# Weight preparation six tiles deep with the third block's attention behind it, and five of the first expert's eight weight pieces behind its gathered rows

## The chip, the cores and the metric

The kernel runs on one NeuronCore of a Trainium2 chip. The metric is the device time of one execution in microseconds (us). The times below are medians of several runs of the same program; the profile is of one more execution. The engines are named as in the profile: PE is TensorE (PEld its weight loads), DVE is VectorE, ACT is ScalarE, POOL is GpSimd and SP is SyncE, which here does nothing but issue DMAs; ACTq and SPq are the DMA issues of ACT and SP.

## What is computed

Three layers follow each other, all in float32 accuracy. The first is gated linear attention, the second a feed-forward layer, the third a mixture of eight experts in which every expert takes exactly 384 of the 3072 tokens:

```python
f = 1.0 / (1.0 + np.exp(-f_logit))                      # 4 batches, 8 heads, 768 steps, 48 wide
for t in range(S):
    state = f[:, :, t, :, None] * state + np.einsum('bhd,bhe->bhde', k[:, :, t], v[:, :, t])
    y[:, :, t] = np.einsum('bhd,bhde->bhe', q[:, :, t], state)
...
h = x @ w_in                                            # 3072 tokens, 384 -> 2048
x = (np.maximum(h, 0) + alpha * np.minimum(h, 0)) @ w_out
...
logits = x @ w_gate                                     # 8 experts, at most N // 8 tokens each
for idx in np.argsort(-logits.flatten()):               # best (token, expert) pairs first
    ...
out[mask] = np.maximum(x[mask] @ w1[e], 0) @ w2[e]      # 384 -> 1024 -> 384
```

## The kernel before

The 3072 tokens are 24 chunks of 128, and three chunks are a block. Attention is done by chunk (`chunk`): on DVE two scans over 128x516 elements (`s1`), two products of 128x512 (`s2`), two maskings of 128x512 (`s3`) and a few small operations; on PE short matmuls between them; the result is a block's input in two halves, high and low (`halve_x`). The feed-forward (`ffn1`) runs by block: for each of 16 hidden chunks nine matmuls (`hidden`), an activation on ACT and DVE, a split into a high and a low half (`split`: ACT rounds, DVE or POOL subtracts), and two chunks later nine matmuls of the projection (`project`). Every product is made of three matmuls (high by low, low by high, high by high).

The weights of the feed-forward come as 64-bit numbers, and are narrowed to 32 bits on the core before they are split: `load_w` loads group g (of 8) into two raw buffers with four DMAs of 384 KB; `prepare_in` and `prepare_out` take two staging tiles each (name "a", three buffers), narrow on ACT and DVE (`narrow`) and split into the weight tiles; `prepare_out` also computes the gate's columns. In the profile, attention buffers and staging tiles are all "early", the prepared weights are "weights", the raw buffers are "raw", the blocks' halves are "rounded".

The order of all engines but for waits is made ahead of time by a planner in the kernel (class `Plan`): the program is recorded as a list of operations with priorities (`at`), and a list scheduler with fixed costs puts them in an order on each engine. `behind(ops)` lets what is recorded in it start only when `ops` have started, and `follow` chains groups of operations in this way; the loads of chunks (c) and weight groups (w) are chained by the string `FIRST`. An operation that may run on DVE or POOL (`low`) goes where the planner sees it end sooner. Where the planner sees a gap on PE, it puts in placeholder matmuls of the constant `ones` (line 1667).

The first blocks' attention, the preparation of the weights and the feed-forward of block 0 overlap. When all weights are prepared, the experts' weights are converted to halves and written to DRAM (`convert`, tensor `wd`), which lies beside the feed-forward of the other blocks. In the last block the hidden part and the logits come first (`ffn1_logits`); then the search for the first expert's tokens (`chain(0)`) runs beside the rows of the last block (`ffn1_rows`), which are stored to the DRAM tensor `x2d`; these three stores are issued by ACT, all others by SP. `expert_weights` reads the chosen expert's number into a register of SP and loads its eight pieces of 768 KB: pieces 0 to 3 are w1 and go into `win`, pieces 4 to 7 are w2. `gather` fetches the expert's 384 rows from `x2d` with three indirect DMAs on POOL, which wait for all rows to be stored; `expert_x` transposes them on PE, and `expert` multiplies: hidden chunks 2i and 2i+1 need piece i, projections 2i and 2i+1 need piece 4+i.

Of the kernel before, what the change touches and what calls it, by code (L numbers as in the profile page):

```python
# [9 lines left out]
F32 = mybir.dt.float32  # L10
F32R = mybir.dt.float32r
BF = mybir.dt.bfloat16
I32 = mybir.dt.int32
# [7 lines left out]
N, DM, DF = B * S, H * D, 2048  # L21
# [8 lines left out]
KD = DM // 128  # L30
# [16 lines left out]
PREP = 15.5  # L47
FFN = 11
CONVERT = 65.0
PART = 65  # L50
LAST = 80.0
CHAIN0 = 81.0
GATHER0 = 80.9
# [14 lines left out]
PLACES = 4  # L68
FILL = 2.0

FIRST = "c0 c1 w0 c2 w1 c3 w2 w3 c4 w4 w5 c5 w6 w7"
LOADS = 2


# [557 lines left out]
class Kernel:  # L632
# [28 lines left out]
    def constants(self, cp):  # L661
        nc = self.nc
        self.cp = cp
        self.ones = cp.tile([128, 128], BF, name="ones")
        with self.at(-4.0):
            nc.vector.memset(self.ones, 1.0)
        jp = self.sp.tile([128, 128], F32, name="a", bufs=3)
        nc.gpsimd.iota(jp, pattern=[[1, 128]], base=0, channel_multiplier=-1,
                       allow_small_or_imprecise_dtypes=True)
        self.ident = cp.tile([128, 128], F32, name="ident")  # L670
        nc.vector.tensor_scalar(self.ident, jp, 0.0, None, op0=OP.is_equal)
        self.mask = cp.tile([128, 128], BF, name="mask")
        nc.vector.tensor_scalar(self.mask, jp, 0.0, None, op0=OP.is_ge)
        self.tri = cp.tile([128, 128], BF, name="tri")
        nc.vector.tensor_scalar(self.tri, jp, 0.0, -1.0, op0=OP.is_le, op1=OP.mult)
        self.pick = cp.tile([2 * E, E], F32, name="pick")
        nc.vector.tensor_tensor(self.pick, self.ident[:2 * E, :E], self.ident[:2 * E, E:2 * E], OP.add)

        self.pairs = cp.tile([128, 128], F32, name="pairs")
        self.turn = cp.tile([128, 2], F32, name="turn")  # L680
        with self.at(PAIRS):
            two = self.sp.tile([128, 128], F32, name="a", bufs=3)
            nc.gpsimd.iota(two, pattern=[[2, 128]], base=0, channel_multiplier=-1, allow_small_or_imprecise_dtypes=True)
            nc.vector.tensor_scalar(self.pairs, two, 0.0, None, op0=OP.is_equal)
            nc.vector.tensor_reduce(self.turn[:, 0:1], self.pairs, axis=AX.X, op=OP.add)
            nc.vector.tensor_scalar(two, two, -1.0, None, op0=OP.is_equal)
            nc.vector.tensor_reduce(self.turn[:, 1:2], two, axis=AX.X, op=OP.add)
            nc.vector.tensor_add(self.pairs, self.pairs, two)
        self.eye8 = cp.tile([E, E], BF, name="eye8")
        nc.vector.tensor_copy(self.eye8, self.ident[:E, :E])  # L690

        self.cols = cp.tile([128, 128, 2], BF, name="cols")
        nc.gpsimd.iota(self.cols, pattern=[[1, 128], [0, 2]], base=0, channel_multiplier=0,
                       allow_small_or_imprecise_dtypes=True)
        nc.vector.tensor_scalar(self.cols, self.cols, -HALF, None, op0=OP.add)

        self.ok = cp.tile([WAYS + 1, 1], BF, name="ok1")
        nc.vector.memset(self.ok, -WAYS / 2.0)


        self.okl = cp.tile([WAYS + 2, E], BF, name="okl")
        nc.gpsimd.iota(self.okl[WAYS:], pattern=[[-1, E]], base=0, channel_multiplier=0, allow_small_or_imprecise_dtypes=True)
        nc.vector.tensor_scalar(self.okl[WAYS:], self.okl[WAYS:], 2.0 ** -13, None, op0=OP.mult)
        nc.vector.memset(self.okl[WAYS:WAYS + 1], -WAYS / 2.0 - 0.5)
        self.wts = cp.tile([128, E], F32, name="wts")
        nc.gpsimd.iota(self.wts, pattern=[[-1, E]], base=E, channel_multiplier=0,
                       allow_small_or_imprecise_dtypes=True)
        self.wtb = cp.tile([128, E], BF, name="wtb")
        nc.vector.tensor_copy(self.wtb, self.wts)
        self.jpv = cp.tile([128, NT, 2], F32, name="jpv")  # L710
        nc.gpsimd.iota(self.jpv[:, :, 0], pattern=[[1, NT]], base=0, channel_multiplier=0,
                       allow_small_or_imprecise_dtypes=True)
        nc.gpsimd.iota(self.jpv[:, :, 1], pattern=[[0, NT]], base=0, channel_multiplier=1,
                       allow_small_or_imprecise_dtypes=True)
        self.lg = cp.tile([128, NT, E], F32, name="lg")
        self.pmin = cp.tile([128, HP], F32, name="state")
        nc.vector.memset(self.pmin, 1.0)
# [89 lines left out]
    def prepare_in(self, g):  # L807

        a = []
        for u in range(2):  # L810
            a.append(self.sp.tile([128, KD, 128], I32, name="a", bufs=3))
            self.narrow(a[u], self.rin[:, u], self.nc.scalar)
        for u in range(2):
            f = 2 * g + u
            self.split(self.in_part(0, f), self.in_part(1, f), a[u].bitcast(F32))

    def prepare_out(self, g):

        a = []
        for u in range(2):  # L820
            a.append(self.sp.tile([128, DM], I32, name="a", bufs=3))
            self.narrow(a[u], self.rout[:, u], self.nc.scalar)
        for u in range(2):
            f = 2 * g + u
            self.split(self.out_part(0, f)[:, :DM], self.out_part(1, f)[:, :DM], a[u].bitcast(F32))
        for u in range(2):
            self.gate(2 * g + u, a[u].bitcast(F32))
# [594 lines left out]
              [w.rearrange("p s a b -> p (s a b)")[:, :4 * DM] for w in self.wo]  # L1422
        return [w.rearrange("p (u s d) -> p u s d", u=2, s=2) for w in own]

    def expert_weights(self, p, ei):

        ts = self.expert_tiles(p)

        def source(i, r):
            return self.wd[ds(r, 1), i].rearrange("o q u s d -> q (o u) s d")  # L1430

        if not self.plan:
            r = self.nc.sync.value_load(ei[0:1, 0:1], min_val=0, max_val=E - 1)
            for i, t in enumerate(ts):
                self.nc.sync.dma_start(t.bitcast(F32), source(i, r))
            return
        reg = []
        get = self.plan.add(("sync",), lambda e, b: reg.append(e.value_load(b(ei[0:1, 0:1]), min_val=0, max_val=E - 1)), [], [ei], 100.0)
        for i, t in enumerate(ts):
            self.plan.add(("sync",), lambda e, b, i=i, t=t: e.dma_start(b(t.bitcast(F32)), source(i, reg[0])), [t], [self.wd], 60.0, 128 * 1536 * 4, [get])  # L1440

    def gather(self, idx):
# [193 lines left out]
    def main(self, ctx):  # L1636
        tc = self.tc
        with ExitStack() as es:
            cp = es.enter_context(tc.tile_pool(name="consts", bufs=1))
            dp = es.enter_context(tc.tile_pool(name="dram", bufs=1, space=DRAM))  # L1640
            self.x2d = dp.tile([N, DM], F32, name="x2d")
            self.wd = dp.tile([E, 8, 128, 2, 2, DM], F32, name="wd")
            self.banks = 3
            self.wide = False
# [29 lines left out]
    def record(self, cp):  # L1674

        nc = self.nc
# [5 lines left out]
        def store(blk):  # L1682
            def put(t, r, logits):
                j = blk * BT + t
                (nc.sync if logits is not None else nc.scalar).dma_start(self.x2d[j * 128:(j + 1) * 128], r)
                if logits is not None:
                    nc.vector.tensor_copy(self.lg[:, j, :], logits)
            return put
# [24 lines left out]
        def attend(b):  # L1713
            with self.at(10.0 * b if b != 1 else ATT1):
                for i in range(b * BT, (b + 1) * BT):
                    self.chunk(i)
                    if i + LOADS < NT:
                        with self.at(10.0 * b - 1):
                            load(i + LOADS)
# [17 lines left out]
        prepared = self.last(1)  # L1737
        self.slack = SLACK
        for b in range(NB - 1):
            attend(b + 1)  # L1740
            if b == 0:
                steps = [loads[x[0], int(x[1:])] for x in FIRST.split()]
                self.plan.follow(steps)
            self.urgent = 10.0 * b + URG
            with self.at(10.0 * b + FFN):
                self.ffn1(self.xT.pop(b), store(b))
        with self.at(CONVERT), self.behind(prepared):
            self.convert()
        with self.at(60.0):
            self.bounds((NB - 1) * BT)  # L1750
        with self.at(PART):
            self.choose(0, NT - BT)
# [6 lines left out]
        self.wide = False  # L1759
        with self.at(CHAIN0):  # L1760
            c = chain(0)
            self.expert_weights(0, c[2])
            idx = self.rp.tile([128, 3], I32, name="idx", bufs=E)
            self.lists(idx, *c[:2])
        listed = self.last(1)
        with self.at(ROWS):
            self.ffn1_rows(G, store(NB - 1))
        with self.at(GATHER0):
            ready = idx, self.expert_x(self.gather(idx))

        self.plan.extra = 3500.0
        with self.at(CHAIN1), self.behind(listed):
# [2 lines left out]
        for p in range(E):  # L1775
# [6 lines left out]
            if p + 1 < E:  # L1782
                with self.at(base + LISTS):
                    idx = self.rp.tile([128, 3], I32, name="idx", bufs=E)
                    self.lists(idx, *was[:2])
                    ready = idx, self.expert_x(self.gather(idx))
# [55 lines left out]
```

## Time and profile before

| | |
|---|---|
| median of three runs | 859.87 us (858.52 to 860.99) |
| the profiled execution | 861.39 us, of which its span 859.5 us |
| PE busy | 825.2 us, 96% of the span |
| DVE busy | 563.2 us, 66% |
| ACT busy | 349.8 us, 41% |
| POOL busy | 121.5 us, 14% |
| DMA | 172.60 MB, mean 201 GB/s |

Busy time is the time in which instructions of an engine ran; for PE it includes the placeholders. A row of the time line gives the start and the length in us, the engine, the line in the code, the operation with what it writes and reads, the number of merged instructions, and in brackets how long the engine stood idle before and what released it. Nearly all operations carry line 210, since the planner issues them from there.

### The profile page before, as it was taken

To read this page: it belongs to the slowest core of one execution; us is meant where nothing else is said; L and a number is where in the kernel's file an instruction comes from. 1 tells how busy PE (TensorE), PEld (TensorE's weight loads), DVE (VectorE), ACT (ScalarE), POOL (GpSimd) and SP (SyncE) were. 2 spreads that over 40 slices of the span, in tenths; PEclk is the share of its full clock that TensorE was granted. 3 is DMA by queue.
4 is the path that set the end of the run, shared out by engine and by line. 5 is a ranking of instruction groups with operands and counts; after the bars stand their busy time and mean duration, and the time that the engine had idled before them with its cause. 6 is when DMAs were issued, how large, how long until landed. Compare 5 with 4: busy or idle time off the path is not lost. (4 is left out here: it accounts for less than half of the span.)

```text
span 859.5 us, 16037 instructions
## 1 busy us (share of the span) xinstructions
PE 825.2 (96%) x6123; PEld 760.2 (88%) x6123; DVE 563.2 (66%) x1301; ACT 349.8 (41%) x742; POOL 121.5 (14%) x112
## 2 busy tenths in 40 slices
PE   7899899999999999999999999998899999999995
PEld 3678789999999999999999999986788898999995
DVE  6898996966966966966866645555667557453220
ACT  2477676455455455455454433410112222212220
POOL 3232410200200200300100001000102212201211
PEclk9899999999999999999999999999899999999998
DMA  8995215789788788898887610007548865777400
GB/s 175 277 251 162 48 29 140 160 281 288 207 286 271 217 281 261 213 308 245 233 266 271 230 76 28 1 10 311 186 175 339 340 248 194 266 278 260 163 27 32
DMA packets 92789, 172.60 MB, mean 201 GB/s; under 512 B 31672, under 2 KB 61376, under 8 KB 92704
## 3 DMA queue, kind: packets, MB, share of 16 engines
q1 hardware_dynamic: 89056, 161.45, 59.1%
q0 software_dynamic: 3072, 9.44, 3.1%
q8 instruction: 50, 0.82, 0.4%
q10 hardware_dynamic: 576, 0.60, 0.2%
q14 instruction: 35, 0.29, 0.1%
HBM read 111.69 MB, written 59.77 MB: 199 GB/s over the span
## 5 line engine op out<-in xcount | busy, mean ns | idle before, releaser
L210 PE MATMUL bank<-rounded,weights 128*128 128x384 f32 (+1 forms) x1740 | 355.5, 345 | 1.4 <-POOL weights L210 1.1
L210 PE MATMUL bank<-weights,rounded 128*128 128x392 f32 (+1 forms) x1620 | 324.0, 344 | 1.5 <-DVE weights L210 0.6
L210 PEld LDWEIGHTS bank<-rounded,weights 128*128 128x128 f32 (+1 forms) x1740 | 303.1, 188 | 8.3 <-issue 2.5
L210 PEld LDWEIGHTS bank<-weights,rounded 128*128 128x128 f32 x1620 | 287.4, 188 | 4.6 <-issue 1.3
L210 ACT ACTIVATE rounded<-bank 128x384 fp32r<-128x384 f32 x110 | 53.9, 491 | 193.9 <-PE bank L210 179.7
L210 DVE TENSOR_TENSOR early<-early 128x384 fp32r<-128x384 f32 (+2 forms) x196 | 119.3, 625 | 11.4 <-ACT early L210 10.9
L210 PEld LDWEIGHTS bank<-early 128*64 128x64 f32 (+2 forms) x1696 | 99.4, 156 | 22.7 <-issue 9.7
L210 PE MATMUL bank<-early 128*64 128x128 f32 (+3 forms) x1696 | 112.0, 272 | 3.7 <-ACT early L210 1.8
L210 DVE SCALAR_TENSOR_TENSOR common<-common,rest,bank 128x384 f32<-128x384 f32 x128 | 77.8, 608 | 52.0 <-ACT common L230 51.6
L210 POOL TENSOR_TENSOR rounded<-common,rounded 128x384 fp32r<-128x384 f32 x35 | 48.1, 1376 | 419.0 <-ACT rounded L210 380.2
L210 ACT ACTIVATE early<-early 128x384 fp32r<-128x384 f32 (+2 forms) x177 | 94.1, 545 | 30.0 <-DMA wd<-early 17.0
L230 ACT ACTIVATE common<-bank 128x384 f32<-128x384 f32 x128 | 62.5, 488 | 85.4 <-PE bank L210 85.2
L210 ACT ACTIVATE rounded<-common 128x384 fp32r<-128x384 f32 x118 | 61.7, 523 | 66.2 <-DVE common L210 66.1
L210 DVE TENSOR_TENSOR rounded<-common,rounded 128x384 fp32r<-128x384 f32 x83 | 47.6, 574 | 30.4 <-ACT rounded L210 22.0
L210 DVE SCALAR_TENSOR_TENSOR rounded<-bank,rounded 128x384 fp32r<-128x384 f32 x62 | 34.5, 556 | 50.3 <-ACT rounded L210 48.9
L210 DVE TENSOR_TENSOR_SCAN early<-early 128x516 f32<-128x516 f32 x48 | 62.7, 1306 | 2.5 <-ACT early L210 2.5
L210 ACT ACTIVATE common<-bank 128x384 f32<-128x384 f32 x48 | 23.2, 491 | 73.3 <-PE bank L210 68.0
L210 POOL DMA_INDIRECT out_dram<-common,late x24 | 24.6, 1023 | 168.9 <-ACT common L210 113.6
L210 DVE TENSOR_TENSOR late<-late,cols 128x1536 bf16<-128x1536 bf16 (+3 forms) x53 | 42.6, 817 | 0.2
L210 POOL DMA_INDIRECT common<-x2d,late x24 | 25.8, 1076 | 97.0 <-DMA weights<-wd 63.8
L210 DVE TENSOR_TENSOR rounded<-bank,rounded 128x384 fp32r<-128x384 f32 x48 | 26.3, 552 | 12.7 <-ACT rounded L210 12.5
L210 DVE TENSOR_TENSOR early<-bank,mask 128x512 f32<-128x512 f32 x48 | 31.3, 684 | 4.7 <-PE bank L210 4.5
(110 smaller groups left out, 499.3 us busy)
## 6 DMA issues: line engine op xcount, KB each, us to landing
wd<-early SPq DMA_DIRECT2D x128, 384.0 KB, 3.6
weights<-wd SPq DMA_DIRECT2D x64, 768.0 KB, 5.6
early<-in_w_dram SPq DMA_DIRECT2D x64, 384.0 KB, 4.4
early<-in_fkq_dram SPq DMA_DIRECT2D x46, 288.0 KB, 4.6
raw<-in_w_in_dram SPq DMA_DIRECT2D x16, 384.0 KB, 9.1
raw<-in_w_out_dram SPq DMA_DIRECT2D x16, 384.0 KB, 7.4
early<-in_v_dram SPq DMA_DIRECT2D x24, 192.0 KB, 3.4
x2d<-common SPq DMA_DIRECT2D x21, 192.0 KB, 2.8
```

What stands on the lines that cost most here:

```text
L210: op = self.add(engines, lambda e, b: getattr(e, method)(*[b(x) for x in a], **{n: b(x) for n, x in k.items()}), outs, ins)
L230: return e.activation(b(out), b(x), AF.Relu, scale=-1.0)
```

## The change

`STAGE` gives the staging tiles six buffers instead of three. `FIRST` moves weight groups 2, 4 and 6 ahead of chunks 3, 4 and 5. The attention of block 2 and later is recorded behind the last operation of the preparation. The first expert's weights are loaded in two parts: pieces 0 to 2 (`AHEAD`) where all stood, and pieces 3 to 7 behind a new DMA of 64 bytes, which reads the third gathered tile and writes it to a DRAM tensor `mark` that nobody reads. That second part reads the expert's number once more. The last block's stores move from ACT to SP.

```diff
-FIRST = "c0 c1 w0 c2 w1 c3 w2 w3 c4 w4 w5 c5 w6 w7"
+AHEAD = 3
+FIRST = "c0 c1 w0 c2 w1 w2 c3 w3 w4 c4 w5 w6 c5 w7"
+STAGE = 6
...
-        jp = self.sp.tile([128, 128], F32, name="a", bufs=3)
+        jp = self.sp.tile([128, 128], F32, name="a", bufs=STAGE)
...
-            a.append(self.sp.tile([128, KD, 128], I32, name="a", bufs=3))
+            a.append(self.sp.tile([128, KD, 128], I32, name="a", bufs=STAGE))
...
-    def expert_weights(self, p, ei):
+    def expert_weights(self, p, ei, part=slice(0, 8)):
...
-        for i, t in enumerate(ts):
+        for i, t in list(enumerate(ts))[part]:
...
+            self.mark = dp.tile([1, 16], F32, name="mark")
...
-                (nc.sync if logits is not None else nc.scalar).dma_start(self.x2d[j * 128:(j + 1) * 128], r)
+                nc.sync.dma_start(self.x2d[j * 128:(j + 1) * 128], r)
...
         for b in range(NB - 1):
-            attend(b + 1)
+            with self.behind(prepared if b else ()):
+                attend(b + 1)
...
-            self.expert_weights(0, c[2])
+            self.expert_weights(0, c[2], slice(0, AHEAD))
...
         with self.at(GATHER0):
-            ready = idx, self.expert_x(self.gather(idx))
+            xg = self.gather(idx)
+
+            nc.sync.dma_start(self.mark, xg[2][:1, :16])
+            here = self.last(1)
+            ready = idx, self.expert_x(xg)
+        with self.at(GATHER0), self.behind(here):
+            self.expert_weights(0, c[2], slice(AHEAD, 8))
```

What this does to the order is shown at two places. The first is DVE where the weights of groups 5 and 6 are prepared; "raw11" to "raw14" are the raw buffers of groups 5 to 7, a 128x516 operation is a scan of the attention, "common<-common,rest" belongs to a hidden chunk. Before:

```order
L210 SCALAR_TENSOR_TENSOR early_110<-raw11_130,early_110 128x384
L210 SCALAR_TENSOR_TENSOR early_110<-raw12_126,early_110 128x384
L210 TENSOR_TENSOR weights11_1199<-early_110,weights11_1199 128x384 x2
L210 SCALAR_TENSOR_TENSOR common_106<-common_106,rest_91,bank7_72 128x384
L210 TENSOR_TENSOR weights9_1058<-bank0_65,weights9_1058 128x2x8
L210 SCALAR_TENSOR_TENSOR early_110<-early_110 128x516
L210 SCALAR_TENSOR_TENSOR early_110<-early_110,raw12_126 128x384
L210 RECIPROCAL early_110<-early_110 128x4
```

And in the changed kernel:

```order
L212 TENSOR_TENSOR weights11_1150<-early_111,weights11_1150 128x384
L212 SCALAR_TENSOR_TENSOR common_107<-common_107,rest_92,bank7_73 128x384
L212 TENSOR_TENSOR weights9_1034<-bank0_66,weights9_1034 128x2x8
L212 SCALAR_TENSOR_TENSOR early_111<-raw12_127,early_111 128x384
L212 SCALAR_TENSOR_TENSOR early_111<-early_111,raw13_123 128x384
L212 TENSOR_TENSOR weights12_1196<-early_111,weights12_1196 128x384 x2
L212 SCALAR_TENSOR_TENSOR early_111<-raw13_123,early_111 128x384
```

The scan and its reciprocal, which belong to block 2, no longer stand between the steps of the weights.

The second place is SP from the last stores of the feed-forward to the pieces of the first expert; TENSOR_LOAD reads the expert's number, "weights" are the pieces in their order 0, 1, 2. Before:

```order
L210 DMA x2d<-common 128x384 x3
L1438 TENSOR_LOAD late
...
L1440 DMA weights_403<-wd 128x1536
...
L1440 DMA weights_591<-wd 128x1536
...
L1440 DMA weights_751<-wd 128x1536
...
L1440 DMA weights_877<-wd 128x1536
```

And in the changed kernel:

```order
L212 DMA x2d<-common 128x384 x4
L1440 TENSOR_LOAD late
...
L1442 DMA weights_419<-wd 128x1536
...
L1442 DMA weights_559<-wd 128x1536
...
L1442 DMA weights_683<-wd 128x1536
L212 DMA x2d<-common 128x384 x2
L212 DMA mark<-common 1x16
L1440 TENSOR_LOAD late
...
L1442 DMA weights_858<-wd 128x1536
```

The stores of the last block stand around the first three pieces; the mark, which reads a gathered tile, stands ahead of the other five.

## Rows read from the trace of the kernel before

**Rows 1.** The page's first part: busy us (share of the span) and instructions.
```profile
PE 825.2 (96%) x6123; PEld 760.2 (88%) x6123; DVE 563.2 (66%) x1301; ACT 349.8 (41%) x742; POOL 121.5 (14%) x112
```

**Rows 2.** Busy time by stretch: from:to, length, each engine (instructions), granted clock, DMA.
```profile
41.70:106.60 64.90, 59.78 (x471) 50.37 (x470) 62.03 (x111) 45.64 (x106) 23.56 (x18) 1.00 0.59 155
106.60:160.00 53.40, 51.55 (x436) 47.15 (x437) 45.14 (x90) 35.30 (x84) 7.77 (x6) 1.00 0.35 92
```

**Rows 3.** The same stretches, the placeholders alone (line 1667): PE and PEld.
```profile
41.70:106.60 64.90, 5.63 (x20) 1.99 (x19) 1.00 0.59 155
106.60:160.00 53.40, 0.39 (x1) 0.10 (x1) 1.00 0.35 92
```

**Rows 4.** Time line of several engines around the gather.
```profile
581.23 0.15 DVE L210 TENSOR_SCALAR late<-taken 128x1 int32<-128x1 f32 x1
...
582.66 9.52 SPq L1440 DMA_DIRECT2D weights<-wd  x8
...
592.75 0.34 ACTq L210 DMA_DIRECT2D x2d<-common  x1
...
600.78 1.12 POOL L210 DMA_INDIRECT common<-x2d,late  x1 [63.75 <-DMA weights<-wd]
...
603.47 0.94 POOL L210 DMA_INDIRECT common<-x2d,late  x1 [0.30 <-issue]
...
603.95 0.90 PE L210 MATMUL bank<-ident,common 128*128 128x128 f32 x3 [4.95 <-DMA common<-x2d,late]
...
607.68 0.85 PE L210 MATMUL bank<-ident,common 128*128 128x128 f32 x3
...
609.54 1.60 PE L210 MATMUL bank<-rounded,weights 128*128 128x384 f32 x6
...
615.18 1.75 PE L210 MATMUL bank<-weights,rounded 128*128 128x384 f32 x9
```

**Rows 5.** PE by stretches of 2.5 us: length, busy, granted clock, DMA share, GB/s.
```profile
597.50:600.00 2.50, 1.50 (x18) 1.00 1.02 420
600.00:602.50 2.50, 0.00 (x0) 1.00 0.27 111
...
605.00:607.50 2.50, 2.50 (x11) 0.50 0.28 79
```

**Rows 6.** DVE by operation, 120 to 150 us, where POOL is nearly idle.
```profile
L210 DVE SCALAR_TENSOR_TENSOR early<-raw,early 128x384 int32<-128x384 int32 x5 | 2.8, 551 | 0.0
...
L210 DVE TENSOR_TENSOR early<-bank,mask 128x512 f32<-128x512 f32 x4 | 2.7, 686 | 0.0
L210 DVE TENSOR_TENSOR_SCAN early<-early 128x516 f32<-128x516 f32 x2 | 2.5, 1227 | 0.0
...
L210 DVE TENSOR_TENSOR early<-early 128x512 f32<-128x512 f32 x2 | 1.4, 680 | 0.0
L210 DVE TENSOR_TENSOR rounded<-common,rounded 128x384 fp32r<-128x384 f32 x2 | 1.1, 558 | 0.8 <-ACT rounded L210 0.7 <-issue 0.2
```

**Rows 7.** POOL by operation, 41.7 to 115 us: count, busy us, mean ns, idle before.
```profile
L210 POOL TENSOR_TENSOR weights<-early,weights 128x384 fp32r<-128x384 f32 x10 | 12.9, 1306 | 24.1 <-ACT weights L210 14.5 <-PE bank L210 9.5
L210 POOL TENSOR_TENSOR rounded<-common,rounded 128x384 fp32r<-128x384 f32 x9 | 12.6, 1397 | 30.6 <-ACT rounded L210 13.9 <-DMA early<-in_fkq_dram 8.3 <-issue 4.5
```

**Rows 8.** DVE by operation, 41.7 to 115 us.
```profile
L210 DVE TENSOR_TENSOR_SCAN early<-early 128x516 f32<-128x516 f32 x10 | 14.4, 1442 | 0.0
L210 DVE SCALAR_TENSOR_TENSOR early<-raw,early 128x384 int32<-128x384 int32 x21 | 13.0, 631 | 0.1
L210 DVE SCALAR_TENSOR_TENSOR early<-early,raw 128x384 int32<-128x384 int32 x21 | 12.3, 610 | 1.7 <-ACT raw L210 1.7
...
L210 DVE TENSOR_TENSOR rounded<-common,rounded 128x384 fp32r<-128x384 f32 x2 | 2.4, 1220 | 0.0
```

**Rows 9.** The page's DMA issues: count, KB each, median us from issue to landing.
```profile
weights<-wd SPq DMA_DIRECT2D x64, 768.0 KB, 5.6
...
x2d<-common SPq DMA_DIRECT2D x21, 192.0 KB, 2.8
```

More of the change, by code (lines that the diff above doesn't have):

```diff
@@ L681, in constants @@
         with self.at(PAIRS):
-            two = self.sp.tile([128, 128], F32, name="a", bufs=3)
+            two = self.sp.tile([128, 128], F32, name="a", bufs=STAGE)
             nc.gpsimd.iota(two, pattern=[[2, 128]], base=0, channel_multiplier=-1, allow_small_or_imprecise_dtypes=True)
@@ L820, in prepare_out @@
         for u in range(2):
-            a.append(self.sp.tile([128, DM], I32, name="a", bufs=3))
+            a.append(self.sp.tile([128, DM], I32, name="a", bufs=STAGE))
             self.narrow(a[u], self.rout[:, u], self.nc.scalar)
```

## The prediction

> **What bounds the kernel now.** I read the share of each engine first, then the same shares by stretch, then the placeholder matmuls, then what stands around the two places where TensorE stops. TensorE is busy for 825 of 859.5 us [rows 1], so only the time in which it waits, or multiplies placeholders into a bank that nobody reads, can be won. There are two such places.
>
> The first is the start. Between 41.7 us, where the feed-forward of block 0 begins, and 106.6 us, where its eleventh hidden chunk begins, TensorE is busy 59.78 of 64.9 us, of which 5.63 us are placeholders [rows 2, 3]: 64.9 - (59.78 - 5.63) = 10.75 us are lost. VectorE is busy 62.03 of the same 64.9 us: it is the bound there, with the attention of block 1, the first scans of block 2 and the preparation of the weights. From 106.6 to 160 us 53.4 - (51.55 - 0.39) = 2.24 us more are lost, and VectorE is idle for 8 us [rows 2, 3].
>
> The second is the step from the feed-forward to the experts. The last rows of x2 leave ScalarE at 592.75 us; the first gather of rows starts only at 600.78 us, 8.0 us later. TensorE runs dry, waits 4.95 us up to 603.95 us, and the first expert's first matmul is at 609.54 us [rows 4]. While the store is under way the DMA engines move 420 GB/s, all but full: the eight pieces of the first expert's weights, issued from 582.66 us on, are in transfer. They fall to 111 GB/s just when the gather starts [rows 4, 5]. The idle time also costs the clock: granted 1.00 up to 602.5 us, 0.50 (1.2 of 2.4 GHz) from 605 us on [rows 5].
>
> **Part 1: six staging tiles, other load order, third block behind the last chunk.** The order of VectorE says what moves. Up to the eleventh hidden chunk it now has 4 scans and 4 products fewer (4 x 1.227 + 4 x 0.680 = 7.6 us, with the small operations between them about 8.2), and 9 splits of weights, 2 splits of hidden chunks and 5 narrowing steps more (16 x 0.555 = 8.9 us) [rows 6]: 0.7 us more work. Up to the sixteenth it is 6 scans, 6 products and 2 masks fewer (12.8 us) against 8 + 3 splits more (6.1 us): 6.7 us less.
>
> The splits come from GpSimd. Ten weight splits and nine hidden ones ran there in this stretch, at 1.31 and 1.40 us [rows 7]; of these 18 stood ahead of the eleventh chunk, and 8 do in the new order. VectorE's operations are longer while they run: against the calm stretch the 10 scans took 1.442 for 1.227 us, the 42 narrowing steps 0.631 and 0.610 for 0.551, the 2 splits 1.220 for 0.558 [rows 6, 8]. That is 2.15 + 1.68 + 1.24 + 1.32 = 6.4 us over 19 GpSimd operations, 0.34 us each; ten fewer give back 3.4 us. The Trainium skill ("SBUF — State Buffer", SBUF: two separate sides) says more: the port pair that VectorE and GpSimd share is locked for a whole instruction and the loser blocks fully. By that ten operations of 1.35 us would give back up to 13.5 us, more than the 13.0 us that can be won here, and the sum below would end near 841 us at the median; the rows show a quarter of it, and I stay with them.
>
> So VectorE reaches the eleventh chunk 3.4 - 0.7 = 2.7 us sooner. TensorE has by then 171 feed-forward matmuls behind it in either order, and a few transposes and attention matmuls less, for which I take off 0.5 us: 2.2 us won. VectorE's own idle time in the stretch is 64.9 - 62.03 = 2.9 us; with six tiles ScalarE need not wait for one to be freed, and I count half, 1.4 us. Behind the eleventh chunk VectorE has some 7 us less to do, but only 2.24 us are lost there; I count 0.8 us, and take 0.4 us off for the attention of block 2, which now stands in one piece behind the preparation. **Together 4.0 us.** The ends: all 13.0 us at one, at the other nothing, if TensorE, which runs in a fixed order, stops at other places instead. On SP's queue chunks 3, 4 and 5 now stand behind one weight group more each; their first scans stand later on VectorE too, behind the splits of those groups, so I price this at nothing, with VectorE's weight work as cover. Without that cover one group, 1.5 MB, is 1.5 / 0.155 = 10 us at the stretch's mean rate [rows 2].
>
> **Part 2: three pieces ahead, five behind the gathered rows; stores on SP.** Pieces 0 to 2 are issued as before at 582.66 us. All eight took until 600 us, so one takes about (600 - 582.7 - 2) / 8 = 1.9 us and three are gone by 591 us, ahead of the last store. That store is then alone: issued at about 593.1 us, landed 2.8 us later [rows 9] at 595.9 us. The gather starts 4.9 us sooner than before. From there I keep the distances of before: the third gather is 2.7 us behind the first and ends 0.94 us later, and its rows land some 2 us on, as the first's did (600.78 + 1.12 to 603.95) [rows 4]: 601.6 us. TensorE, which is done with the rest at 599.0 us (4.95 us ahead of 603.95), finds the first rows at 599.1 us, waits for little, and keeps the clock at 1.00. From the third transposes to the first expert it was 609.54 - 607.68 = 1.86 us [rows 4]; the expert then starts at 603.4 us. **6.1 us won, I take 6.0.** The ends: 4.9 us from the gather alone if the clock falls all the same, less if the pieces come late (below); 7.0 us if the 1.86 us, which ran at half the clock, halve as well.
>
> What the new wait holds up: the mark's DMA waits on SP for the third gather, and behind it stand a second load of the expert's number, the five pieces and all of expert 1's weights. Loading the number took at most 582.66 - 581.38 = 1.3 us before [rows 4], so the pieces are issued from 601.6 + 0.3 + 1.3 = 603.2 us on. The second of them is the first that TensorE needs (piece 4, for the first projection); at the median of 5.6 us from issue to landing [rows 9] it is there at 608.8 us. The first projection stood 615.18 - 609.54 = 5.6 us behind the first expert matmul [rows 4]; now a fourth hidden chunk (nine matmuls, 1.6 us) stands ahead of it, so it is due at 603.4 + 7.2 = 610.6 us. That is 1.8 us of slack, and this is the thinnest cover of the change: every us beyond it is lost again. Expert 1's pieces follow directly, but nothing needs them before the first expert is through. That the stores are issued by SP and not by ScalarE costs nothing: ScalarE has little to do there, and SP's queue is empty between the third piece and the mark.
>
> **The sum.** The profiled execution took 861.39 us, of which its span is 859.5 and 1.9 us lie around it; it stands 1.5 us above the median of the three runs, 859.87. Nothing behind 610 us has less work, and TensorE is the bound there, so both gains should stay: 861.4 - 4.0 - 6.0 = 851.4 us for such an execution, 849.9 us at the median. I predict 850.
>
> **The rivals.** (a) Only the gather gains. TensorE's order is fixed, and a stop at one weight may only move to the next, or to the first attention matmuls of block 2. For it: VectorE's work up to the eleventh chunk hardly changes. Against it: GpSimd's ten operations. 854 us.
>
> (b) The gather comes no sooner. Then its 8.0 us are not the pieces' doing: a store that is slow by itself, or a wait for something else. For it: the page has no landing time for the stores on ScalarE's queue. Against it: the gather starts within 1 us of the moment at which the weights' transfer ends [rows 4, 5]. The time would be 856 us. The Trainium skill ("DMA: Bandwidth & Descriptors", Queues, rings and completion order) speaks for this rival: each DMA engine goes round its queues packet by packet, so a store on a queue of its own should pass pieces queued on another, and moved to SP's queue it would stand behind them instead. By that, nothing is won before, and the move to SP costs only if pieces were left, which at 591 us they are not.
>
> (c) The held pieces come late. If the pieces move at half the rate, piece 4 lands 2 x 1.9 = 3.8 us later and TensorE waits 2.0 us at the first projection; if the clock falls for it as it did at 602.5 us, some 2 us more: 854 us. For it: gathers and pieces share the engines. Against it: at that moment nothing else is in transfer.
>
> (d) Slower. The third block's attention, held until the last chunk is begun, meets TensorE's order with nothing prepared. Each of its three chunks needs two scans, two products and two masks on VectorE (2.45 + 1.36 + 1.37 = 5.2 us [rows 6]) between TensorE's steps; if TensorE stands for all three, that is 15.6 us, 865.5 us with both gains. It decides once more than 10 us of them are open. For it: all three stand close together in the new order. Against it: 84 feed-forward matmuls stand between them there, 16 us at 1.75 us for nine [rows 4], which cover them if VectorE starts in time.
>
> **How the numbers follow.** The forecast has 0.62, (a) 0.15, (b) 0.08, (c) 0.08, no change that shows 0.04, (d) 0.03. The range of the forecast itself is 845 to 855; 844.5 to 856.5 leaves out part 1 near its best end, (d) and most of "no change". A measurement of this kernel can tell about 0.3%, 2.6 us, from no change. Faster by more: all of the forecast, (a), (c) and nearly all of (b), 0.92. Within it: 0.05. Slower: 0.03.
>
> **What would show it.** Part 1 is right if TensorE's loss from the feed-forward's start to 160 us falls from 13.0 to about 9 us, with fewer GpSimd operations and shorter scans beside them; wrong if the loss stays, or shows up at the masks of block 2. Part 2 is right if the gather starts about 3 us behind the last store, TensorE has no wait over 1 us there, the granted clock stays at 1.00 and the first projection does not wait for a DMA; (b) is right if those 8 us stay. The prediction as a whole is wrong if the first expert is not some 10 us earlier, or if it is and the end is not.

## The result and the profile after

The changed kernel takes 850.04 us, the median of four runs (846.21 to 853.12); the kernel before took 859.92 us beside it (858.52 to 860.99). The ratio is 0.9884, 95% interval 0.9839 to 0.9929: 10.0 us less, 6 to 14 us. The profiled execution took 851.19 us, its span 849.3 us.

The page's first part, against [rows 1]: TensorE is busy 5.2 us less in a span 10.2 us shorter, and GpSimd has 105 instructions for 112.

```profile
PE 820.0 (97%) x6122; PEld 756.5 (89%) x6122; DVE 564.8 (66%) x1308; ACT 349.6 (41%) x742; POOL 113.9 (13%) x105
```

The start, busy time by stretch (all engines; then clock, DMA share, GB/s), against [rows 2]. The feed-forward begins at 41.76 us (41.70 before). Its eleventh hidden chunk ends at 103.00 us; the first stretch of [rows 2] ends where that chunk begins.

```profile
41.76:103.00 61.24, 57.42 (x467) 50.69 (x466) 59.62 (x117) 43.50 (x104) 9.98 (x8) 1.00 0.66 177
...
103.00:160.00 57.00, 54.56 (x432) 50.30 (x432) 44.56 (x85) 33.29 (x79) 7.16 (x7) 1.00 0.24 66
```

The same stretches, placeholders alone, against [rows 3].

```profile
41.76:103.00 61.24, 4.26 (x16) 1.57 (x16) 1.00 0.66 177
...
103.00:160.00 57.00, 0.00 (x0) 0.00 (x0) 1.00 0.24 66
```

TensorE loses 61.24 - (57.42 - 4.26) = 8.08 us and then 2.44 us, 10.5 us together, where it lost 13.0. GpSimd has 8 operations in the first stretch, 18 before.

The step to the experts, time line of the engines (from, length, engine, operation, idle before), against [rows 4].

```profile
579.43 1.55 SPq L1442 DMA_DIRECT2D weights<-wd  x3
581.08 8.77 SPq L212 DMA_DIRECT2D x2d<-common  x2
588.99 0.49 ACT L212 ACTIVATE common<-bank 128x384 f32<-128x384 f32 x1 [8.78 <-PE bank L212]
592.43 1.12 POOL L212 DMA_INDIRECT common<-x2d,late  x1 [58.56 <-DVE late L212]
595.84 0.49 PE L212 MATMUL bank<-ident,common 128*128 128x128 f32 x3
598.14 0.28 SPq L212 DMA_DIRECT2D mark<-common  x1
598.48 0.49 PE L212 MATMUL bank<-ident,common 128*128 128x128 f32 x3
599.50 13.32 SPq L1442 DMA_DIRECT2D weights<-wd  x13
599.75 1.41 PE L212 MATMUL bank<-rounded,weights 128*128 128x384 f32 x6
606.79 0.93 PE L212 MATMUL bank<-weights,rounded 128*128 128x384 f32 x4
619.52 0.87 PE L212 MATMUL bank<-ident,common 128*128 128x128 f32 x3 [1.88 <-DMA common<-x2d,late]
```

The last rows leave ScalarE at 589.48 us, the gather starts 2.95 us later (8.0 before), TensorE meets the rows without a wait and begins the first expert at 599.75 us, 9.8 us sooner than before. Of these, 3.2 us were there when the pieces were first issued (579.43 for 582.66), so 6.6 us are won at the gather. TensorE by stretches, against [rows 5]:

```profile
597.50:600.00 2.50, 2.46 (x26) 1.00 0.02 9
600.00:602.50 2.50, 2.50 (x16) 1.00 0.81 235
...
605.00:607.50 2.50, 2.50 (x16) 1.00 1.02 423
...
620.00:622.50 2.50, 2.50 (x11) 0.50 1.01 414
```

The clock now stays at 1.00 where it fell to 0.50. It falls later, at 620 us, behind the 1.88 us that TensorE waits for the second expert's rows.

### The profile page after: what moved, and what is told of

The parts are those of the page before. It is cut to its first block, busy times and chain, and to the rows that moved or that the text cites. A ratio compares the mean times of both kernels' runs of the same rounds, so it can differ in the third digit from the quotient of the medians.

```text
span 849.3 us, 16038 instructions
## 1 busy us (share of the span) xinstructions
PE 820.0 (97%) x6122; PEld 756.5 (89%) x6122; DVE 564.8 (66%) x1308; ACT 349.6 (41%) x742; POOL 113.9 (13%) x105
## 5 line engine op out<-in xcount | busy, mean ns | idle before, releaser
L212 PE MATMUL bank<-early 128*64 128x128 f32 (+3 forms) x1696 | 110.2, 269 | 2.7 <-DVE early L212 1.5
L212 DVE TENSOR_TENSOR rounded<-bank,rounded 128x384 fp32r<-128x384 f32 x48 | 26.3, 555 | 10.8 <-ACT rounded L212 10.3
```

The source lines that it names most:

```text
L212: op = self.add(engines, lambda e, b: getattr(e, method)(*[b(x) for x in a], **{n: b(x) for n, x in k.items()}), outs, ins)
```

## Experiments

The change has two parts that can be separated: no instruction of the start depends on the pieces, and the order of VectorE in the start is the same with or without part 2. A gain below is (1 - ratio) times the median of the kernel before on the same chip (855.94 us for the first four, 856.05 for the next four, 857.53 for the last four). Beside the times stands a measure from the trace, the **start**: from the feed-forward's first matmul to the issue of the first expert piece, 582.66 - 41.70 = 540.96 us before and 579.43 - 41.76 = 537.67 us after. It leaves out the first 40 us, whose length (39.3 to 41.8 us with the changed kernel's start) differs between executions of the same order. A stretch in which the granted clock falls to 0.50 is still in it, and it is said where there is one.

**Part 1 alone.**

```diff
-                nc.sync.dma_start(self.x2d[j * 128:(j + 1) * 128], r)
+                (nc.sync if logits is not None else nc.scalar).dma_start(self.x2d[j * 128:(j + 1) * 128], r)
...
-            self.expert_weights(0, c[2], slice(0, AHEAD))
+            self.expert_weights(0, c[2])
...
-            nc.sync.dma_start(self.mark, xg[2][:1, :16])
...
-            self.expert_weights(0, c[2], slice(AHEAD, 8))
```

> Part 1 alone: six staging tiles, the new load order, the third block behind the preparation; all eight pieces ahead of the gather and the last stores on ScalarE, as in the kernel before. In the changed kernel the search for the first expert begins 3.2 us earlier, and TensorE's loss from the feed-forward's start to 160 us is 10.5 instead of 13.0 us. Theory (both parts gain, and add): 3.2 us, 856.7 us, the gather still 8.0 us behind the last rows. Rival (the start gives nothing that lasts, the whole gain is the gather's): 859.9 us. Rival (the start holds the 4.0 us of the prediction or more): 855.9 us or less.

Ratio 0.9955 (0.9939 to 0.9971): 3.9 us, 2.5 to 5.2. The start is 537.61 us. The gather has its long distance still; ACT, POOL and PE in its time line:

```profile
588.49 0.49 ACT L212 ACTIVATE common<-bank 128x384 f32<-128x384 f32 x1 [8.78 <-PE bank L212]
597.18 1.12 POOL L212 DMA_INDIRECT common<-x2d,late  x1 [63.91 <-DMA weights<-wd]
600.51 0.90 PE L212 MATMUL bank<-ident,common 128*128 128x128 f32 x3 [5.24 <-DMA common<-x2d,late]
605.74 1.30 PE L212 MATMUL bank<-rounded,weights 128*128 128x384 f32 x6
```

From the last rows (588.98) to the gather 8.2 us, to the first expert 16.8 us.

**Part 2 alone.** Without six tiles, load order and held third block:

```diff
-FIRST = "c0 c1 w0 c2 w1 w2 c3 w3 w4 c4 w5 w6 c5 w7"
-STAGE = 6
+FIRST = "c0 c1 w0 c2 w1 c3 w2 w3 c4 w4 w5 c5 w6 w7"
+STAGE = 3
...
-            with self.behind(prepared if b else ()):
-                attend(b + 1)
+            attend(b + 1)
```

> Part 2 alone: three pieces ahead, five behind the third gathered tile, the last stores on SP; the start as in the kernel before. Theory (both parts gain, and add): 6.5 us, 853.4 us, the gather 2.9 us behind the last rows, the first expert 6.5 us earlier than before, the granted clock at 1.00 there. Rival (what is won at the gather needs the earlier start, since the pieces must be gone in time): the gather again about 8 us behind the rows, near 859 us. Rival (the start gives nothing): 850 us.

Ratio 0.9927 (0.9899 to 0.9955): 6.2 us, 3.9 to 8.6. The start is 540.83 us, as before, and the gather as after the change:

```profile
589.96 0.49 ACT L212 ACTIVATE common<-bank 128x384 f32<-128x384 f32 x1 [8.78 <-PE bank L212]
593.38 1.12 POOL L212 DMA_INDIRECT common<-x2d,late  x1 [58.59 <-DVE late L212]
600.32 1.39 PE L212 MATMUL bank<-rounded,weights 128*128 128x384 f32 x6
```

2.9 us to the gather, 9.9 us to the first expert. The parts add: 3.9 + 6.2 = 10.1 us.

**The queue of the last stores.** First all eight pieces ahead with the stores behind them on SP (the diff of part 1 alone without its first two lines), then the changed kernel with the stores back on ScalarE (those two lines alone).

> The changed kernel without holding pieces back: all eight pieces ahead on SP's queue, the last two stores behind them on the same queue. Theory (the pieces' bytes fill the engines, whichever queue the store is on): the gather 8 us behind the last rows as before, and the time of part 1 alone, 856.7 us. Rival (a queue of its own lets the store pass pieces, so moving it behind them costs): the gather 10 us behind the rows or more, 859 us or more. Rival (the move to SP is itself what helps): the gather 3 us behind, 850 us.

> The changed kernel with the last block's stores back on ScalarE; five pieces are still held behind the gathered rows. Theory (only the bytes in transfer matter, the store's queue does not): the gather 3 us behind the last rows and 850.0 us as the changed kernel. Rival (the store needs SP's queue): the gather 5 to 8 us behind, 853 to 857 us.

Eight ahead on SP: 0.9983 (0.9966 to 1.0), 1.5 us. Held pieces with the stores on ScalarE: 0.9873 (0.9845 to 0.99), 10.9 us, the gather 589.88 - 586.94 = 2.94 us behind the rows, as with the stores on SP. The last store by itself, with its median us from issue to landing (one store each): of part 1 alone, of eight ahead on SP, of part 2 alone, and of held pieces with the stores on ScalarE.

```profile
x2d<-common ACTq DMA_DIRECT2D x1, 192.0 KB, 7.2
x2d<-common SPq DMA_DIRECT2D x1, 192.0 KB, 11.2
x2d<-common SPq DMA_DIRECT2D x1, 192.0 KB, 1.9
x2d<-common ACTq DMA_DIRECT2D x1, 192.0 KB, 1.9
```

So the bytes of the pieces delay the store: with no piece under way it lands after 1.9 us on either queue. With pieces under way its queue counts too: 7.2 us on ScalarE's queue, 11.2 us behind the pieces on SP's. With eight ahead on SP the rows left at 591.11 us. TensorE by stretches of 1 us, DMA share and GB/s last, and under them the gather:

```profile
598.00:599.00 1.00, 0.74 (x6) 1.00 0.98 353
599.00:600.00 1.00, 1.00 (x7) 1.00 0.21 78
...
601.00:602.00 1.00, 1.00 (x8) 1.00 0.14 41
```

```profile
603.64 1.23 POOL L212 DMA_INDIRECT common<-x2d,late  x1 [68.15 <-DVE inc L212]
```

Most of the transfers are over at 599 us, but the last of them go on, at a small share, to about 602 us, and the store lands at 602.36 us. The gather follows 1.28 us later, where the other kernels have 1.0 to 1.1 us; a scan on VectorE that ends at 603.60 us released it. That is 12.5 us behind the rows, so the rival's distance (10 us or more) is what came. Its time (859 us or more) is not: this kernel lost 2.4 us against part 1 alone and still gained 1.5. In part 1 alone the store landed at 596.17 us, 3.0 us ahead of the last piece. So the move to SP by itself costs 4.0 us at the store where pieces are ahead of it, and nothing where they are held.

**Which piece of part 1.** Four kernels, each with part 2 as in the changed kernel: without the held third block; with it alone; tiles alone; load order alone.

```diff
-            with self.behind(prepared if b else ()):
-                attend(b + 1)
+            attend(b + 1)
```

> The changed kernel without holding the third block's attention behind the preparation: six staging tiles, the new load order and the held pieces stay. In this order 18 scans stand among the weights again (12 in the changed kernel), and GpSimd has 19 splits of the first block and the weights (24 before, 13 in the changed kernel). Theory (the order on VectorE, scans out of the weights' way and fewer GpSimd operations, is the gain of part 1): most of its 3.4 to 3.9 us go, ratio to the kernel before 0.991 to 0.993. Rival (tiles and load order are the gain): 0.987 to 0.9885, as the changed kernel.

```diff
-FIRST = "c0 c1 w0 c2 w1 w2 c3 w3 w4 c4 w5 w6 c5 w7"
-STAGE = 6
+FIRST = "c0 c1 w0 c2 w1 c3 w2 w3 c4 w4 w5 c5 w6 w7"
+STAGE = 3
```

> The changed kernel with three staging tiles and the old load order; the third block stands behind the preparation, the pieces are held. 12 scans stand among the weights, GpSimd has 17 splits there. Theory: most of part 1's gain stays, ratio to the kernel before 0.988 to 0.990. Rival (tiles and load order are the gain, and without them the held block only leaves VectorE waiting): 0.992 to 0.995.

The next two are the first of these diffs, with the old `FIRST` (tiles alone) or with `STAGE = 3` (order alone).

> Of part 1 only the six staging tiles: load order and third block as in the kernel before, pieces held as in the changed kernel. From the feed-forward's first matmul to the first piece of the expert's weights it was 541.0 us in the kernel before, 537.7 in the changed one and without the held third block too. Theory (weights can be prepared when they arrive, tiles are what lacked): 537.7 to 538.5 us, ratio to the kernel before 0.988 to 0.990. Rival (the load order did it): 540.5 to 541 us, 0.992 to 0.993, as part 2 alone. Third (each gives a part): in between.

> Of part 1 only the new load order, with three staging tiles and the third block as before; pieces held as in the changed kernel. Theory (tiles are what lacked): 540.5 us or more from the feed-forward's first matmul to the first piece, ratio 0.992 to 0.994. Rival (the load order did it): 537.7 to 538.5 us, 0.988 to 0.990.

| part 1 has | ratio (95%) | start, us |
|---|---|---|
| nothing (part 2 alone) | 0.9927 (0.9899 to 0.9955) | 540.83 |
| third block held alone | 0.9943 (0.9923 to 0.9963) | 541.67 |
| tiles alone | 0.9940 (0.9917 to 0.9963) | 544.77, clock 0.78 from 80 to 103 us |
| order alone | 0.9966 (0.9943 to 0.9990) | 543.60 |
| tiles and order | 0.9888 (0.9867 to 0.9910) | 538.50, clock 0.50 from 108.8 to 112.2 us |
| all three, again | 0.9875 (0.9848 to 0.9902) | 541.09, clock 0.66 from 65 to 80 us |

My theory fell: holding the third block gives nothing that shows, with the other two or alone. Tiles and order together shorten the start by 2.3 us against part 2 alone, in a trace that has 3.4 us at half the clock. The order alone makes the start 2.8 us longer. What the tiles do alone stays open: the clock was at 0.50 for 10.3 us of that start, which is at most 5.1 us of its 544.77, and their time shows no gain either (0.9940), but the ten runs lie between 848.4 and 856.9 us. These kernels ran on different chips, and 2 to 3 us are as fine as the comparison goes. That tiles without weights, or weights without tiles, leave VectorE nothing to do is a reading of it; no run tested it.

**GpSimd beside VectorE.** All splits of the weights and the first block on VectorE:

```diff
-SLACKW = 0
+SLACKW = -1000000
...
             self.urgent = 10.0 * b + URG
+            self.slack = SLACK if b else -1000000
```

> The changed kernel with all splits of the weights and of the first block on VectorE; GpSimd has none of the 13 that it has there in the changed kernel. Theory (a GpSimd operation lengthens VectorE's by 0.34 us): VectorE is relieved of 13 x 0.34 = 4.4 us and gets 13 x 0.56 = 7.3 us more to do; the start is 1 to 3 us longer, ratio 0.990 to 0.992. Rival (VectorE stands still for a GpSimd operation, 1.1 to 1.6 us each): relieved of 15 to 18 us, the start is shorter by up to the 8 us that TensorE still loses, ratio 0.979 to 0.984.

Ratio 0.9906 (0.9884 to 0.9928), start 540.11 us, 2.44 us longer than the changed kernel's, as forecast (1 to 3 us). Its feed-forward begins at 38.03 us instead of 41.76, so that a part of this may be only the earlier first matmul. VectorE by operation from 41.7 to 115 us, of the changed kernel (10 GpSimd operations beside it), and then of this one (none):

```profile
L212 DVE SCALAR_TENSOR_TENSOR early<-early,raw 128x384 int32<-128x384 int32 x25 | 15.9, 654 | 0.0
L212 DVE SCALAR_TENSOR_TENSOR early<-raw,early 128x384 int32<-128x384 int32 x25 | 14.0, 582 | 0.0
L212 DVE TENSOR_TENSOR weights<-early,weights 128x384 fp32r<-128x384 f32 x23 | 13.6, 609 | 1.6 <-ACT weights L212 1.3
L212 DVE TENSOR_TENSOR_SCAN early<-early 128x516 f32<-128x516 f32 x6 | 7.8, 1294 | 0.2 <-ACT early L212 0.2
...
L212 DVE TENSOR_TENSOR rounded<-common,rounded 128x384 fp32r<-128x384 f32 x4 | 3.0, 740 | 0.0
L212 DVE TENSOR_TENSOR early<-early 128x384 f32<-128x384 f32 x3 | 2.4, 797 | 0.0
```

```profile
L212 DVE TENSOR_TENSOR weights<-early,weights 128x384 fp32r<-128x384 f32 x24 | 12.7, 552 | 0.7 <-ACT weights L212 0.5
L212 DVE SCALAR_TENSOR_TENSOR early<-raw,early 128x384 int32<-128x384 int32 x23 | 12.3, 554 | 0.0
L212 DVE SCALAR_TENSOR_TENSOR early<-early,raw 128x384 int32<-128x384 int32 x23 | 12.1, 554 | 1.2 <-ACT raw L212 1.2
L212 DVE TENSOR_TENSOR_SCAN early<-early 128x516 f32<-128x516 f32 x6 | 7.4, 1226 | 0.0
L212 DVE TENSOR_TENSOR rounded<-common,rounded 128x384 fp32r<-128x384 f32 x13 | 7.2, 555 | 0.3 <-ACT rounded L212 0.2
L212 DVE TENSOR_TENSOR early<-early 128x384 f32<-128x384 f32 x3 | 1.6, 548 | 1.4 <-PE bank L212 1.4
```

Without GpSimd each operation has its calm length of [rows 6]. So the lengthening is GpSimd's doing. In the changed kernel it is 25 x 0.10 + 25 x 0.03 + 23 x 0.057 + 6 x 0.068 + 4 x 0.185 + 3 x 0.25 = 6.4 us over 10 operations, 0.64 us each. A split costs VectorE 0.55 us, so by these rows moving one there would neither win nor lose much; that the start became longer, and by how much of this, they do not explain. The Trainium skill ("SBUF — State Buffer", SBUF: two separate sides) has the loser blocked for the whole instruction; by that, 10 operations of 1.11 us (8) and 1.56 us (2) would cost up to 12 us, by estimate. The rows show about half of it, and the start did not get shorter.

**The second expert's rows.** Five, then all eight of the second expert's pieces behind its own gathered rows; the last two kernels ran beside each other, the second being the changed kernel again.

```diff
-            self.expert_weights(1, nxt[2])
+            self.expert_weights(1, nxt[2], slice(0, AHEAD1))
...
-                    ready = idx, self.expert_x(self.gather(idx))
+                    xg = self.gather(idx)
+                    if p == 0:
+                        nc.sync.dma_start(self.mark1, xg[2][:1, :16])
+                        here = self.last(1)
+                    ready = idx, self.expert_x(xg)
+                if p == 0:
+                    with self.at(base + LISTS), self.behind(here):
+                        self.expert_weights(1, was[2], slice(AHEAD1, 8))
```

`AHEAD1` is 3; where all eight are held it is 0 and the first call is gone.

> The changed kernel, and in the same way five of the second expert's eight pieces behind its own gathered rows. In the changed kernel TensorE waits 1.88 us at 619.5 us for those rows, which are gathered while 21 pieces are in transfer, and the granted clock is 0.50 for 2.5 us behind it. Theory (the pieces ahead delay the rows): the wait goes, and with it most of the time at half the clock, 1.9 + 1.2 = 3.1 us less than the changed kernel, ratio to the kernel before 0.985. Rival (the five pieces then come late for the second expert, which starts 15 us behind the wait): the wait moves to its projections, 0 to 3 us more than the changed kernel, 0.9885 to 0.992.

> The changed kernel with all eight pieces of the second expert behind its own gathered rows; the orders of all engines but SP are those of the changed kernel. With three of them ahead the engines still moved 410 GB/s when the second gather ran, and TensorE waited 1.5 us. Theory (the engines must be empty at the gather): the five pieces of the first expert are through at about 610 us, the gather starts at 610.8 us and meets none; the wait of 1.88 us and 2.5 us at half the clock go, 3.1 us less than the changed kernel, ratio to the kernel before 0.985. Rival (eight pieces issued only at 617 us, 1.9 us each, come late at the second expert's start at 634.7 us or its projections): TensorE waits for weights there, as the changed kernel or up to 3 us more, 0.988 to 0.992.

> The changed kernel once more, on the same chip as the three others, so that they can be compared with it. Theory: ratio to the kernel before 0.987 to 0.989, 537.7 us from the feed-forward's first matmul to the first piece, gather 2.9 us behind the last rows.

Five held: 0.9901 (0.9883 to 0.9919); TensorE still waits 1.47 us for the rows, since eight pieces stand in transfer at the gather. All held: 0.9871 (0.9844 to 0.9898) beside 0.9875 (0.9848 to 0.9902) of the changed kernel. There the wait is gone and the clock holds; TensorE by stretches:

```profile
610.00:612.50 2.50, 2.50 (x26) 1.00 0.25 57
...
615.00:617.50 2.50, 2.50 (x19) 1.00 0.13 47
...
620.00:622.50 2.50, 2.50 (x16) 1.00 1.01 415
```

From the first gather to the end of the span it is 843.9 - 591.87 = 252.0 us, against 849.1 - 593.36 = 255.7 us of the changed kernel beside it. That does not show that the edit pays: the latter trace also has a wait of 1.06 us for pieces at the first projection, and the kernel with held pieces and the stores on ScalarE, which does not hold the second expert's, takes 841.4 - 589.88 = 251.5 us. The medians (845.95 and 846.25 us) show no difference, within 2 to 3 us. No version is shown to beat the changed kernel.

## Why the prediction held, and where its steps did not

**The sum** (10.0 us) came out at 10.0, and both of its parts within their intervals: part 1 4.0 forecast, 3.9 alone on the chip (3.3 by the start in the traces); part 2 6.0 forecast, 6.2 alone (6.6 in the trace). Rivals (a) and (b), only the gather or only the start, fall with the two kernels that each have one part. (d) falls too: the kernel without the held block is no faster, so holding it costs nothing that shows.

**Part 1 was right in size and wrong in its steps.** The first term, 10 GpSimd operations fewer at 0.34 us, was 3.4 us. Two groups of VectorE's operations were left out of its price: 12 weight splits (666 against 552 ns) and five small operations of the attention:

```profile
L210 DVE TENSOR_TENSOR state<-state,early 128x4 f32<-128x4 f32 x5 | 2.4, 475 | 0.0
```

Without GpSimd these last take 137 ns. With both, the kernel before lost 6.4 + 1.4 + 1.7 = 9.5 us to 19 operations, 0.50 each; after it is 6.4 us over 10, 0.64 each. The relief is 3.1 us, near the 3.4, but by luck: the price was too low, and it is not fixed. The stretch itself was read 1.7 us short: at 106.6 us the eleventh chunk begins in the kernel before, with 162 feed-forward matmuls done and not 171. It is through at 108.34 us, with 66.64 - (61.46 - 5.63) = 10.81 us lost:

```profile
41.70:108.34 66.64, 61.46 (x480) 1.00 0.58 153
```

There the loss fell by 10.81 - 8.08 = 2.7 us where I had 3.6. Behind it I expected 0.4 us more; TensorE lost 0.3 more up to 160 us, and 0.7 us in a wait for GpSimd's split at 280 to 300 us that was not there before. That makes 1.8 of the 3.3 us. The other 1.5 us are no idle time: the same matmuls are busy that much shorter, and why stays open. So the loss fell from 13.0 to 10.5 us, not to 9, which the prediction gave as the sign of part 1. And of three edits I named the wrong one as a source: the scans moved behind the weights were counted as relief, and the kernel that leaves them among the weights is as fast within the noise.

**Part 2 was right in its path.** From rows to gather 3.1 us were forecast and 2.95 measured, and that close only by luck: the store alone landed after 1.9 us and not 2.8, and the gather followed 1.05 us behind the landing where I had nothing. TensorE did not wait at the transposes, the clock stayed at 1.00, and the first expert began 9.8 us sooner. The mis-sized term is the cover of the held pieces. They were forecast to be issued 0.2 us ahead of the first expert's start and were 0.25 us ahead; the first projection was due 7.4 us behind their issue and stood 7.3 us behind it; but I let piece 4 land after 5.6 us, by the median of all 64 pieces [rows 9]. It needs more: in five of eleven traces with held pieces TensorE waited there, 0.3 to 1.4 us. The kernel without the held block:

```profile
606.21 0.97 PE L212 MATMUL bank<-weights,rounded 128*128 128x384 f32 x4 [1.44 <-DMA weights<-wd]
...
619.40 0.55 PE L212 MATMUL bank<-ident,common 128*128 128x128 f32 x3 [2.31 <-DMA common<-x2d,late]
```

Its pieces were issued at 597.74 us, so the weights were there 8.5 us later. The slack of 1.8 us was none there. So rival (c) is right that the pieces can come late, and its price was too high: the longest wait is 1.4 us, and the clock did not fall for it. What I did not see is the next line of the chain: with the first expert 10 us sooner the second gather still runs among the pieces, and its wait (0.43 and 1.60 us before, 1.88 now) can go on costing the clock: behind it the clock fell in four of ten traces with the first expert's pieces held (waits of 1.47 to 2.31 us) and stayed in the other six (0.59 to 1.54 us).

**The rule on queues.** The Trainium skill ("DMA: Bandwidth & Descriptors", Queues, rings and completion order) lets each DMA engine go round its queues by packets, which was rival (b)'s ground. The rows bear it out in part. With eight pieces on SP's queue a store on ScalarE's landed 7.2 us after its issue, 3.0 us ahead of the last piece, and 11.2 us after it where it stood behind them on SP's. But it did not pass them freely, since it takes 1.9 us with none under way. So what the rival drew from it, that nothing is to be won at the gather, did not come.

## What to carry to other kernels

A short transfer that someone waits for is best protected by not issuing the long ones: a tiny DMA that reads the awaited tile, ahead of them in the same queue, does it, and the cover behind it has to be taken from when the last held piece lands under load, not from the median of all. Where long ones have to be ahead, a queue of its own saved the short one 4 us here. An edit that feeds an engine may show nothing alone (the load order here), so test it together with the one that it needs before dropping it. When the gain is as large as forecast, undo each edit all the same: one of three here did nothing that shows.

## What was not expected of the hardware

The granted clock can fall or not at the same place of the same order. TensorE by stretches in the second trace of the changed kernel, and under it the same stretches of its first:

```profile
65.00:67.50 2.50, 2.09 (x25) 1.00 0.66 150
67.50:70.00 2.50, 1.80 (x12) 0.74 1.01 284
70.00:75.00 5.00, 5.00 (x21) 0.50 0.93 252
```

```profile
65.00:67.50 2.50, 2.50 (x49) 1.00 0.41 97
67.50:70.00 2.50, 2.08 (x25) 1.00 0.64 149
70.00:75.00 5.00, 4.31 (x32) 1.00 1.02 330
```

In both, TensorE stops 0.4 us for VectorE and 0.69 us for ScalarE between short attention matmuls, some 2.5 us sooner in the second trace. There the clock then goes to 0.50 (1.2 of 2.4 GHz) until about 79 us, and the start is 541.09 us instead of 537.67, 3.4 us longer. It fell in two of the seven traces with this order of the start: 541.1 and 541.3 us there, 537.5 to 538.2 us in the five others. This may be a good part of the spread of the result: its four runs come in the order of their mean granted clock, 846.21 us at 0.995, 848.88 at 0.991, 851.19 at 0.989 and 853.12 at 0.984. In which stretches the clock fell in the runs that were not traced is not known.
